# Eight row buffers for V in place of six, with a new instruction order, in a fused adaLN block of sliding attention and SwiGLU

## The chip, the cores and the metric

The kernel runs on one core of a Trainium2 chip. Five engines work beside one another and are ordered by semaphores alone: TensorE (PE in the profile, with its weight loads as PEld), VectorE (DVE), ScalarE (ACT), GpSimd (POOL) and SyncE (SP), which here issues nearly all DMA transfers. The metric is the device time of one execution in microseconds (us), the median of several runs.

## The reference

A transformer block on x of 2048 rows and 512 columns, in bfloat16, modulated by a conditioning vector c:

```python
mod = (silu(c) @ w_mod).reshape(1, 6, 1, 512)
sa, ca, ga, sb, cb, gb = mod[:, 0], ..., mod[:, 5]
h = layernorm(x) * (1 + ca) + sa
x = x + ga * attention(h)              # @ wqkv, window, @ wo
h = layernorm(x) * (1 + cb) + sb
x = x + gb * ((silu(h @ w1) * (h @ w3)) @ w2)   # 512 -> 1792 -> 512
return x
```

The attention has 32 heads of 16 columns. Row s attends to the eight rows s, s − 2, ..., s − 14, those before row 0 masked, with a softmax over the eight.

## The kernel before

The rows lie in 16 tiles of 128, T = 0 to 15. One function, `_build`, records 1151 operations of all engines by number in the program's own order. Two tables then fix how they run. `ORDER` is a list of those numbers; split by engine, it is the order in which each engine executes its operations, and for SP the order in which transfers are issued. `SLOTS` gives, for each of 590 values that live in a pool of buffers, which buffer of the pool it takes. `Program.place` goes through `ORDER`, and where a value takes a buffer that another had, its first operation must wait for every user of the value before (`o.prev`). `Program.synchronize` turns these and the data dependences into semaphore waits. Nothing waits otherwise: an engine runs its list from first to last, and an operation that waits holds up all that stand behind it on that engine.

The pools that matter here: eight PSUM banks of 512 columns, which all products on TensorE share, three buffers for modulated rows `h`, four output buffers, and `vpool`, the row buffers `vb` for V.

The work, in groups that overlap:

- LayerNorm 1 and the projections to q, k and v go in row groups {0,1}, {2,3}, {4–7}, {8–11}, {12–15}. After the statistics, TensorE transposes the rows and ScalarE evacuates them with the modulation (line 673); for the last group a DMA transposes. Keys and queries come out transposed (product at line 722, evacuation on ScalarE at 730 to 734).
- V comes out with rows on the partitions (`proj_v`, line 749). A copy on ScalarE (line 759) reorders its columns into a buffer of `vpool`, and a DMA of 128 KB on SP stores that buffer into a scratch tensor in HBM, `v_scratch_dram`. The buffer can be written again when the store has landed.
- Attention goes by tile. VectorE multiplies q by eight shifted views of k (line 780); TensorE sums over each head's columns (line 791, in 32-column tiles of the array); the softmax runs on VectorE (803 to 840) with the exponential on ScalarE (821). Four DMA loads per tile (`values`) bring the eight shifted rows of V back from the scratch tensor, VectorE weights them (line 862), TensorE sums over the window (line 871), ScalarE copies the sum out (877), a DMA transposes it, TensorE multiplies by wo (895), and VectorE adds the result to x (899).
- LayerNorm 2 takes a square with accumulation on ScalarE (614), two small operations on GpSimd (620, 621), one on VectorE (622) and the normalization on ScalarE (625). DMA transposes it and ScalarE modulates it in place (648); for the first groups TensorE transposes.
- The feed-forward network goes in the same row groups, numbered 0 to 4. For each of 14 blocks f of 128 hidden columns TensorE makes a gate and an up product (line 911, four matmuls each), ScalarE takes silu of the gate (917) and, in groups 0 to 3, copies the up product out (921), and VectorE multiplies (922; from PSUM in group 4, line 925). The product with w2 (953; 941 for the last two tiles) and the addition on VectorE (969) end it, and a DMA stores the rows.

ScalarE holds one table of functions at a time: exp and silu each need a table load (ACT_TABLE_LOAD) where they follow the other. Both orders have eight loads.

The operation numbers that the text speaks of:

| operations | engine | what |
|---|---|---|
| 153, 159, 203, 207, 254, 257, 260, 263, 312, 315, 318, 321, 366, 369, 372, 375 | ACT | copies of V of tiles 0 to 15; each one's store is the next number, on SP |
| 403–406, 413–416 | SP | loads of the shifted V rows of tiles 0 and 1 |
| 49, 45, 44 | SP | weight load w3 (second part), gate and scale weights of the second modulation |
| 293, 294 and 295 | ACT, PE | last modulated rows of tiles 8 to 11; the first key product of tiles 12 to 15 behind them |
| 542, 543 | PE, ACT | window sum of tile 9, its copy out |
| 553 | ACT | exponential of the logits of tiles 10 and 11 |
| 911, 871, 881, 883, 866, 876, 873 | PE | gate and up products of FFN group 2 |
| 912, 884, 882 | ACT | silu of 911; up copy and silu of 883 and 881 |
| 1014, 1004 | ACT | up copies of group 3, f = 10 and f = 8 |
| 1057, 1062, 1061 | ACT | square of tile 15; normalization of tiles 15 and 14 |
| 1066, 1065, 826 | SP | the last two transposes of FFN group 4's rows; a store of output rows of tile 3 |

Of the kernel before, what the change touches and what calls it, by code (L numbers as in the profile page):

```python
# [10 lines left out]
P = 128  # L11
S = 2048
D = 512
# [267 lines left out]
def _build(p, A_x, A_wqkv, A_wo, B_w1, B_w3, B_w2, c, w_mod, out):  # L281
# [6 lines left out]
    def sb(shape, dtype, name):  # L288
        return ctx.enter_context(nc.sbuf_tensor("sb_" + name, shape, dtype))
# [11 lines left out]
    vb = [sb([P, D], bf, f"v{i}") for i in range(6)]  # L301
# [761 lines left out]
]  # L1063
SLOTS = [
# [45 lines left out]
```

## Time and profile before

| | before |
|---|---|
| median of 3 runs | 238.87 us (238.83 to 239.16) |
| the profiled execution | 239.86 us |
| its span in the profile | 237.7 us |
| granted clock of TensorE | 1.00 |
| instructions in the trace | 4314 |
| busy: PE, DVE, ACT, POOL | 229.9, 169.8, 156.4, 23.1 us |
| the sixteen stores of V, issue to landing | 3.0 at least, 5.8 median, 12.3 at most |

How to read it: the page counts an engine busy while an instruction runs and lists for each idle stretch what released it. A row of the timeline is start, duration, engine, line and operation, output <- inputs with shapes, the number of instructions merged into the row, and in square brackets the idle time ahead of it with its releaser. A row of the waits is the waiting engine and line, what it waited for, and then us in total, times and the longest. Each time in the text is of that one execution unless it says otherwise.

### The profile page before, as it was taken

How to read it: one execution, taken by the hardware profiler on the slowest of the kernel's cores; microseconds unless marked ns; L12 is line 12 of the kernel's file. 1: busy time of each engine (PE TensorE's matmuls, PEld its weight loads, DVE VectorE, ACT ScalarE, POOL GpSimd, SP SyncE). 2: the span in 40 equal slices, each digit the busy share in tenths (PEclk: the TensorE clock that was granted, in tenths of full speed). 3: DMA queues.
4: the chain of work that ended last, by engine and by line, in shares of the span. 5: the costliest groups of instructions: out<-in, count | busy, mean ns of one | idle time of the engine just before them, and what ended most of it. 6: DMA issues, size and time to landing. Idle time of an engine off the chain costs nothing.

```text
span 237.7 us, 4314 instructions
## 1 busy us (share of the span) xinstructions
PE 229.9 (97%) x1665; PEld 120.7 (51%) x1689; DVE 169.8 (71%) x284; ACT 156.4 (66%) x311; POOL 23.1 (10%) x55
## 2 busy tenths in 40 slices
PE   7899998999999999999999999999999999999996
PEld 2667543544568855754434444444344444444454
DVE  4789998999999999999999847379134424042722
ACT  2289798899989987683689799444757926133100
POOL 8323050001001000030000021000001100000000
PEclk9999999999999999999999999999999999999999
DMA  6999999989999977693897484330032142000002
GB/s 185 341 352 351 238 274 179 188 221 297 327 261 273 285 181 223 139 261 69 205 330 116 124 229 105 103 117 0 3 90 88 44 77 80 0 0 0 3 0 88
DMA packets 44731, 38.31 MB, mean 161 GB/s; under 512 B 19736, under 2 KB 36008, under 8 KB 44712
## 3 DMA queue, kind: packets, MB, share of 16 engines
q1 hardware_dynamic: 44656, 38.04, 63.3%
q8 instruction: 13, 0.21, 0.4%
q14 instruction: 6, 0.05, 0.1%
q10 hardware_dynamic: 56, 0.01, 0.0%
HBM read 29.63 MB, written 4.21 MB: 142 GB/s over the span
## 4 chain that ended last, share of the span: by engine, by line
PE 68%; DVE 12%; DMA 7%; ACT 7%; issue 3%; POOL 1%; SPq 1%; DVEq 0%
PE pall L911 38%; PE pall L953 13%; PE pall L722 5%; DMA sb_wo<-in_A_wo_dram 5%; PE pall L895 4%; DVE sb_vsh L862 3%; PE pall L941 3%; DMA sb_wm_s<-in_w_mod_dram 2%; PE pall L871 2%; PE pall L749 2%; ACT sb_h L648 1%; ACT sb_xn L614 1%; PE pall L791 1%; DVE sb_pq L780 1%; DVE sb_pq L862 1%
## 5 line engine op out<-in xcount | busy, mean ns | idle before, releaser
L911 PE MATMUL pall<-sb_h,sb_w 128*128 128x512 bf16 (+1 forms) x554 | 99.6, 336 | 0.5 <-issue 0.2
L911 PEld LDWEIGHTS pall<-sb_h,sb_w 128*128 128x128 bf16 x560 | 52.2, 98 | 47.1 <-ACT sb_sg L917 5.2
L917 ACT ACTIVATE sb_sg<-pall 128x512 bf16<-128x512 f32 (+1 forms) x70 | 33.9, 516 | 29.6 <-PE pall L911 28.6
L953 PE MATMUL pall<-sb_w,sb_hh 128*128 128x512 bf16 x190 | 43.4, 379 | 0.3
L722 PE MATMUL pall<-sb_h,sb_wqkv 128*128 128x512 bf16 (+1 forms) x157 | 30.4, 336 | 1.3 <-ACT sb_v L759 0.8
L953 PEld LDWEIGHTS pall<-sb_w,sb_hh 128*128 128x128 bf16 x196 | 18.9, 98 | 22.7 <-issue 0.4
L921 ACT ACTIVATE sb_hh<-pall 128x256 bf16<-128x256 f32 (+1 forms) x56 | 26.8, 497 | 3.4 <-PE pall L911 3.0
L922 DVE TENSOR_TENSOR sb_hh<-sb_sg,sb_hh 128x256 bf16<-128x256 bf16 (+1 forms) x56 | 17.7, 351 | 12.8 <-ACT sb_hh L921 12.8
L969 DVE TENSOR_TENSOR sb_o<-pall,sb_x 128x512 bf16<-128x512 f32 (+3 forms) x18 | 10.9, 627 | 18.5 <-PE pall L953 13.7
L722 PEld LDWEIGHTS pall<-sb_h,sb_wqkv 128*128 128x128 bf16 x160 | 14.6, 98 | 14.0 <-ACT sb_v L759 1.3
L925 DVE TENSOR_TENSOR sb_hh<-sb_sg,pall 128x512 bf16<-128x512 bf16 x14 | 9.1, 684 | 16.0 <-PE pall L911 15.9
L648 ACT ACTIVATE sb_h<-sb_h,sb_modc 128x512 bf16<-128x512 bf16 x16 | 11.7, 806 | 11.2 <-DMA sb_h<-sb_xn 11.2
L620 POOL TENSOR_SCALAR sb_rs<-sb_var 128x2 f32<-128x2 f32 x8 | 3.4, 427 | 144.4 <-ACT sb_xn L614 144.4
L862 DVE TENSOR_TENSOR sb_pq<-sb_pq,sb_al 128x4096 bf16<-128x4096 bf16 x7 | 15.8, 2285 | 1.0 <-DMA sb_pq<-v_scratch_dram 1.0
L862 DVE TENSOR_TENSOR sb_vsh<-sb_vsh,sb_al 128x4096 bf16<-128x4096 bf16 x7 | 15.9, 2281 | 0.0
L749 PE MATMUL pall<-sb_wqkv,sb_h 128*128 128x512 bf16 x59 | 15.2, 379 | 0.3 <-issue 0.2
L895 PE MATMUL pall<-sb_wo,sb_ot 128*128 128x512 bf16 x60 | 14.9, 379 | 0.6 <-issue 0.5
L673 ACT ACTIVATE sb_h<-pall,sb_modc 128x256 bf16<-128x256 bf16 (+1 forms) x20 | 12.2, 659 | 2.7 <-DVE sb_modc L522 1.8
L780 DVE TENSOR_TENSOR sb_vsh<-sb_q,sb_kT 128x4096 bf16<-128x4096 bf16 x6 | 13.6, 2286 | 0.4 <-ACT sb_q L730 0.4
L625 ACT ACTIVATE sb_xn<-sb_x,sb_nb,sb_rs 128x512 bf16<-128x512 bf16 x16 | 12.4, 818 | 1.9 <-DVE sb_nb L622 1.7
L614 ACT ACTIVATE sb_xn<-sb_x,sb_nm 128x512 bf16<-128x512 bf16 x16 | 11.4, 716 | 2.7 <-DVE sb_nm L610 2.7
L899 DVE SCALAR_TENSOR_TENSOR sb_x<-pall,sb_x 128x512 bf16<-128x512 f32 x16 | 10.7, 678 | 2.9 <-PE pall L895 2.7
(111 smaller groups left out, 254.5 us busy)
## 6 DMA issues: line engine op xcount, KB each, us to landing
sb_pq<-v_scratch_dram SPq DMA_DIRECT2D x28, 256.0 KB, 6.8
sb_vsh<-v_scratch_dram SPq DMA_DIRECT2D x28, 256.0 KB, 5.0
sb_w<-in_B_w_dram SPq DMA_DIRECT2D x6, 512.0 KB, 6.9
sb_w<-in_B_w_dram SPq DMA_DIRECT2D x6, 384.0 KB, 5.9
v_scratch_dram<-sb_v SPq DMA_DIRECT2D x16, 128.0 KB, 5.8
out_dram<-sb_o SPq DMA_DIRECT2D x14, 128.0 KB, 1.8
sb_wqkv<-in_A_wqkv_dram SPq DMA_DIRECT2D x6, 256.0 KB, 6.2
sb_x<-in_A_x_dram SPq DMA_DIRECT2D x3, 512.0 KB, 7.7
```

The lines of the kernel that those rows point to most:

```text
L614: p.op("act", lambda e, vn=vn, T=T: e.activation(vn.at[:], x_sb[:, T, :], ACT.Square, bias=nm[:, T, :], scale=D ** -0.5, accum_out=var[:, ...
L648: return e.activation(vh.at[:, ft, 0:n * P], vh.at[:, ft, 0:n * P], ACT.Identity, bias=modc[:, 8 * which + ft:8 * which + ft + 1], scale=m ...
L722: ins = e.matmul(bank(vp)[:, 0:n], wqkv[:, t, kind * D + ft * P:kind * D + (ft + 1) * P], vh.at[:, t, 0:n], start=(t == ORDER[0]), stop=(t ...
L749: ins = e.matmul(bank(vp), vh.at[:, t, tt * P:(tt + 1) * P], wqkv[:, t, 2 * D:3 * D], start=(t == ORDER[0]), stop=(t == ORDER[-1]))
L780: return e.tensor_tensor(bass.AP(vp.at, 0, [[8 * D, P], [KT * P, W], [P, KT], [1, P]]), in0, in1, ALU.mult)
L862: return e.tensor_tensor(v_w, v_w, a_w, ALU.mult)
L895: ins = e.matmul(bank(vy), vt.at[:, ft, :], wo[:, ft, :], start=(ft == 0), stop=(ft == KT - 1))
L911: ins = e.matmul(bank(vp)[:, 0:n], wt[:, t, fi * P:(fi + 1) * P], vh.at[:, t, 0:n], start=(t == 0), stop=(t == KT - 1))
L917: p.op("act", lambda e: e.activation(vt.at[:, 0:n], bank(vgp)[:, 0:n], ACT.Silu), c_act(n), k, r=[vgp], w=[vt], table="silu")
L921: p.op("act", lambda e: e.activation(vh_.at[:, 0:n], bank(vup)[:, 0:n], ACT.Copy), c_act(n), k, r=[vup], w=[vh_])
L922: p.op("dve", lambda e: e.tensor_tensor(vh_.at[:, 0:n], vt.at[:, 0:n], vh_.at[:, 0:n], ALU.mult), 60 + n * 69 // 128, k, r=[vt], w=[vh_], ...
L953: ins = e.matmul(bank(vz), vhh[fi].at[:, tt * P:(tt + 1) * P], w2[:, fi, :], start=(fi == 0), stop=(fi == NF - 1))
```

## The change

The list of V buffers has eight entries in place of six, and `ORDER` and `SLOTS` are replaced whole by another search's result, for which the landings of those stores had been put longer. The operations recorded are the same 1151 in both, and so are their shapes; only the order on each engine and the buffer of each value differ. The copies of V run in the tile order 1, 0, 2, 3, 7, 4, 6, 9, 10, 5, 8, 11, 14, 13, 12, 15 before the change and 1, 0, 2, 4, 6, 3, 7, 9, 5, 11, 10, 8, 14, 13, 12, 15 after it.

```diff
-    vb = [sb([P, D], bf, f"v{i}") for i in range(6)]
+    vb = [sb([P, D], bf, f"v{i}") for i in range(8)]
...
 ORDER = [
...
-    212, 209, 150, 151, 217, 155, 156, 152, 157, 175, 158, 159, 153, 109, 114, 9, 180, 181, 154, 41, 49, 210, 192, 129, 195, 186, 187, 160,
-    44, 198, 130, 201, 182, 218, 40, 144, 405, 220, 265, 188, 145, 45, 267, 42, 266, 139, 202, 203, 146, 147, 213, 183, 184, 140, 185, 196,
-    197, 199, 404, 148, 141, 221, 193, 194, 131, 132, 133, 134, 200, 416, 214, 215, 216, 226, 225, 222, 224, 228, 223, 227, 230, 189, 177,
...
-    208, 262, 263, 264, 248, 284, 392, 394, 393, 39, 283, 290, 291, 395, 425, 286, 287, 292, 250, 288, 294, 326, 327, 239, 240, 293, 204,
-    396, 335, 397, 398, 54, 252, 243, 241, 242, 423, 237, 238, 254, 245, 295, 314, 399, 384, 259, 336, 400, 337, 338, 340, 339, 328, 401,
-    297, 343, 329, 330, 341, 331, 402, 385, 417, 260, 261, 303, 299, 379, 315, 301, 380, 305, 300, 342, 52, 407, 302, 244, 246, 381, 344,
...
-    613, 614, 993, 625, 626, 936, 1047, 924, 973, 1049, 990, 974, 1048, 994, 1050, 1027, 1051, 995, 985, 1010, 1052, 1013, 966, 968, 975,
-    969, 1054, 637, 1022, 967, 627, 628, 1023, 1024, 928, 1003, 638, 1012, 1055, 1028, 1064, 1056, 1057, 1058, 1059, 970, 1053, 1039, 1035,
-    1043, 1031, 1025, 1063, 1014, 1004, 1060, 1062, 1066, 826, 1061, 1029, 1015, 1065, 1070, 1069, 1030, 1005, 1036, 1044, 1037, 1068, 1032,
...
+    172, 157, 109, 126, 209, 119, 201, 202, 152, 186, 158, 42, 114, 124, 159, 160, 180, 211, 210, 219, 212, 198, 217, 153, 154, 41, 45, 181,
+    44, 182, 183, 184, 139, 405, 185, 134, 416, 187, 213, 214, 220, 189, 195, 192, 188, 203, 193, 194, 218, 221, 135, 406, 40, 413, 144,
+    199, 200, 222, 267, 215, 231, 145, 146, 196, 197, 147, 216, 226, 223, 233, 225, 224, 234, 148, 232, 235, 227, 404, 415, 276, 274, 265,
+    275, 277, 278, 414, 279, 228, 229, 205, 206, 129, 190, 236, 177, 130, 136, 137, 266, 230, 131, 132, 133, 403, 178, 140, 334, 141, 142,
+    268, 269, 270, 143, 377, 179, 191, 138, 259, 253, 254, 247, 323, 325, 378, 280, 241, 249, 271, 273, 272, 282, 289, 49, 54, 284, 260,
+    290, 250, 242, 332, 392, 281, 394, 393, 283, 243, 248, 425, 395, 396, 285, 244, 207, 208, 291, 286, 287, 288, 245, 292, 294, 326, 335,
...
+    548, 551, 581, 542, 731, 535, 543, 552, 825, 373, 536, 560, 571, 727, 553, 554, 561, 569, 911, 912, 871, 728, 881, 570, 370, 826, 883,
+    884, 866, 882, 876, 568, 873, 874, 872, 891, 555, 556, 877, 557, 582, 885, 868, 869, 562, 376, 630, 544, 584, 892, 851, 893, 861, 863,
...
+    962, 963, 964, 1009, 1054, 1064, 1011, 998, 1012, 965, 1010, 1053, 1063, 924, 999, 1013, 1001, 1018, 1019, 1000, 1002, 1003, 1043, 1014,
+    1015, 1020, 1004, 1035, 1005, 1036, 732, 1039, 1040, 1057, 1058, 1059, 1060, 1062, 1066, 1041, 1061, 1065, 1069, 1067, 1037, 1031, 1032,
...
 SLOTS = [
...
```

99 rows, old and new, of tables (ORDER, SLOTS) are left out of this document.

## The prediction, made before the changed kernel was built

> **What bounds the kernel now.** I read the head of the page first, then the share of the engines in seven stretches, then the waits and the stretches around the longest of them. The head says how full each engine is, and the page's fourth part what the chain that ends last consists of.
>
> ```profile
> span 237.7 us, 4314 instructions
> PE 229.9 (97%) x1665; PEld 120.7 (51%) x1689; DVE 169.8 (71%) x284; ACT 156.4 (66%) x311; POOL 23.1 (10%) x55
> PE 68%; DVE 12%; DMA 7%; ACT 7%; issue 3%; POOL 1%; SPq 1%; DVEq 0%
> ```
>
> TensorE is busy for 229.9 of 237.7 us, so all that any reordering can win is 7.8 us, and most of that lies where no buffer of V plays a part: in the next table 2.34 us before 14 us and 2.48 us after 199 us. Its columns are the stretch, its length, the busy time of PE, PEld, DVE, ACT and POOL, the granted clock, the DMA share and GB/s.
>
> ```profile
> 0.00:14.00 14.00, 11.66 (x105) 6.08 (x106) 7.77 (x29) 4.98 (x10) 7.05 (x27) 1.00 0.88 276
> 14.00:42.00 28.00, 26.94 (x228) 15.80 (x230) 26.48 (x46) 24.81 (x50) 6.93 (x12) 1.00 1.12 273
> 42.00:62.00 20.00, 19.69 (x227) 10.44 (x229) 19.63 (x22) 18.85 (x37) 1.23 (x2) 1.00 1.03 250
> 62.00:116.00 54.00, 52.99 (x479) 34.75 (x486) 52.93 (x83) 42.40 (x101) 3.85 (x6) 1.00 0.89 215
> 116.00:157.00 41.00, 40.68 (x225) 17.75 (x229) 30.07 (x53) 31.90 (x54) 2.15 (x4) 1.00 0.69 179
> 157.00:199.00 42.00, 41.68 (x214) 17.89 (x217) 19.74 (x36) 25.78 (x48) 1.85 (x4) 1.00 0.21 46
> 199.00:237.70 38.70, 36.22 (x193) 18.00 (x194) 13.15 (x22) 7.71 (x14) 0.00 (x0) 1.00 0.07 24
> ```
>
> From 42 to 116 us VectorE is as full as TensorE (19.63 of 20 and 52.93 of 54), so time must be won on both there. After 116 TensorE alone is full, with 0.32 us idle in each of two stretches. ScalarE is full only from 42 to 62 (18.85 of 20). What the V buffers cost now stands in the waits, and in the timeline around 38 us:
>
> ```profile
> DVE sb_pq L862 <- DMA sb_pq<-v_scratch_dram: 1.0, 1, 1.0
> ACT sb_v L759 <- DMA v_scratch_dram<-sb_v: 0.8, 1, 0.8
> PE pall L722 <- ACT sb_v L759: 0.8, 1, 0.8
> ```
> ```profile
> 37.64 4.49 DVE L862 TENSOR_TENSOR sb_pq<-sb_pq,sb_al 128x4096 bf16<-128x4096 bf16 x2 [1.01 <-DMA sb_pq<-v_scratch_dram]
> ...
> 39.56 0.60 ACT L759 ACTIVATE sb_v<-pall 128x512 bf16<-128x512 f32 x1 [0.84 <-DMA v_scratch_dram<-sb_v]
> ...
> 40.21 1.90 PE L722 MATMUL pall<-sb_h,sb_wqkv 128*128 128x512 bf16 x8 [0.80 <-ACT sb_v L759]
> ```
>
> One copy of sixteen waits for a store: that of V tile 9, whose buffer still feeds the store of tile 7, and the key projection behind it waits 0.80 us for the bank. Beside it VectorE waits 1.01 us for the shifted V rows of tile 1. These two are what the change can remove.
>
> **The change, part by part.** *The buffers.* Two more buffers are memory and cost no time. Followed through the new buffer numbers, tile 9's copy waits for no store, nor does that of tile 10. But tiles 4 and 6 now come early and wait for the stores of tiles 0 and 1; eight buffers therefore don't end the waits, they move them. Eight copies now reuse a buffer whose store must have landed, where ten did. Copies and stores stay sixteen each.
>
> *The V loads at the start.* SP issues in order. These are the rows of its queue, of the stores, and of the copies (count | busy, mean ns | idle before):
>
> ```profile
> 16.35 0.58 SPq L127 DMA_DIRECT2D sb_w<-in_B_w_dram  x1
> ...
> 22.54 4.45 SPq L127 DMA_DIRECT2D sb_pq<-v_scratch_dram  x7
> ```
> ```profile
> v_scratch_dram<-sb_v SPq DMA_DIRECT2D x16, 128.0 KB, 5.8
> ```
> ```profile
> DMA to landing us min/median/max: 3.0/5.8/12.3
> ```
> ```profile
> L759 ACT ACTIVATE sb_v<-pall 128x512 bf16<-128x512 f32 x16 | 9.7, 613 | 2.2 <-PE pall L749 1.3 <-DMA v_scratch_dram<-sb_v 0.8
> L917 ACT ACTIVATE sb_sg<-pall 128x512 bf16<-128x512 f32 x42 | 24.1, 597 | 27.9 <-PE pall L911 27.9
> ```
>
> In the old order a weight load (op 49, issued at 16.35) goes ahead of all eight V loads of tiles 0 and 1; in the new one it goes behind them. The loads then land earlier, and I take the whole wait on VectorE as gone: −1.0, between −1.01 and 0 (0 if the stores, now tile 1 before tile 0 at SP, set the loads' start). The store wait at tile 9 lies on TensorE in a stretch where VectorE is just as full, so beside the −1.0 it gives 0, at the most −0.8. Next late on VectorE is then the residual addition of tile 1, behind this product, which the change doesn't move forward on TensorE:
>
> ```profile
> 48.41 1.89 PE L895 MATMUL pall<-sb_wo,sb_ot 128*128 128x512 bf16 x8
> ```
>
> It may give part of the −1.0 back; the terms that follow stand for that. Of the stores, that of tile 7 (264) falls from place 35 to 65 in SP's queue. The first load that reads it stands 13 places on; at 0.6 of SP's time each (the 0.58 row) that is 7.8 us, more than the median landing of 5.8, so 0 here.
>
> *ScalarE before 42 us.* Ahead of the last modulated rows of tiles 8 to 11 (op 294) stand two V copies (254, 260) and two key evacuations more and one V copy (263) less: 1.93 us by their own durations. The gaps there that could take it up are these:
>
> ```profile
> 27.25 0.60 ACT L759 ACTIVATE sb_v<-pall 128x512 bf16<-128x512 f32 x1 [0.40 <-PE pall L749]
> ...
> 29.22 0.78 ACT L673 ACTIVATE sb_h<-pall,sb_modc 128x512 bf16<-128x512 bf16 x1 [0.89 <-PE pall L663]
> ```
>
> 0.40 + 0.89 = 1.29, which leaves 0.64 for TensorE's key projection (295) to wait; between 0 and +0.64, I take +0.4, as the copies are also pulled out of later ScalarE work. The copy 254 now comes where ScalarE stood at 23.4 us; a store issued like tile 1's at 17.0 lands by the median at 17.0 + 5.8 = 22.8, by the longest at 29.3. Early by 0.6 or late by 5.9: I take +0.3, close to the median. By 115 us the sum is −1.0 + 0.4 + 0.3 = −0.3.
>
> *FFN group 2 (tiles 4 to 7).* This is the largest cost I find. The rows at its start:
>
> ```profile
> 112.94 2.93 ACT L648 ACTIVATE sb_h<-sb_h,sb_modc 128x512 bf16<-128x512 bf16 x4 [3.47 <-DMA sb_h<-sb_xn]
> ...
> 114.50 0.62 PE L791 MATMUL pall<-sb_vshx,sb_E 128*32 128x256 bf16 x16 [0.28 <-DVE sb_vshx L780]
> ...
> 115.93 2.33 PE L911 MATMUL pall<-sb_h,sb_w 128*128 128x512 bf16 x10
> ```
>
> Now TensorE enters the group at 115.93, 0.06 after ScalarE's last modulation (112.94 + 2.93 = 115.87). In the new order its first gate (911) takes the bank of the attention sum of tile 9 (542), and the copy that empties it (543) is queued on ScalarE behind that modulation. One copy, 0.60, and the hand-over of 0.06 come on top: 0 if the modulation ends that much before TensorE is ready, +0.66 if not. VectorE's product for tile 9 is now the last before it, at the place of the 114.50 row, so TensorE isn't ready early; I take +0.5. Behind 543 stand the exponential (553) and both table loads:
>
> ```profile
> 86.42 1.28 ACT L821 ACT_TABLE_LOAD   x1
> 87.71 0.58 ACT L821 ACTIVATE pall<-pall 128x512 f32<-128x512 f32 x1
> 88.30 1.28 ACT L917 ACT_TABLE_LOAD   x1
> ```
> ```profile
> 157.18 9.07 PE pall L911 x42
> ```
>
> 1.28 + 0.58 + 1.28 + three evacuations of 0.60 make 4.94 us from the end of copy 543. TensorE issues six products of four matmuls at 9.07/42 = 0.216, that is 6 × 0.864 = 5.18 us, before it needs the bank of the third one freed. So that costs nothing, with 0.24 to spare.
>
> The Trainium skill (ScalarE: Activation LUTs, What ACT_TABLE_LOAD costs) puts a switch of tables at 1283 ns of load and a drain of 1380 ns behind it. The trace shows the 1.28, and the exponential 1.29 after the load began, so no drain of that size is exposed here; by the page the 4.94 would be 7.70 and the sum 2.5 us higher.
>
> *FFN groups 3 and 4.* The rows around the last group's start:
>
> ```profile
> 188.28 2.86 SPq L127 DMA_TRANSPOSE sb_h<-sb_xn  x2
> 191.18 0.58 SPq L127 DMA_DIRECT2D out_dram<-sb_o  x1
> 191.80 1.20 SPq L127 DMA_TRANSPOSE sb_h<-sb_xn  x1
> ```
> ```profile
> 186.74 0.72 ACT L614 ACTIVATE sb_xn<-sb_x,sb_nm 128x512 bf16<-128x512 bf16 x1
> ...
> 188.15 1.07 ACT L921 ACTIVATE sb_hh<-pall 128x512 bf16<-128x512 f32 x2
> 189.10 1.52 ACT L625 ACTIVATE sb_xn<-sb_x,sb_nb,sb_rs 128x512 bf16<-128x512 bf16 x2
> ...
> 195.82 2.93 ACT L648 ACTIVATE sb_h<-sb_h,sb_modc 128x512 bf16<-128x512 bf16 x4 [4.71 <-DMA sb_h<-sb_xn]
> ```
> ```profile
> 198.81 1.47 PE L911 MATMUL pall<-sb_h,sb_w 128*128 128x512 bf16 x6
> ```
>
> The last group's rows are ready at 195.82 + 2.93 = 198.75 and TensorE starts at 198.81: no slack. In the new order the two evacuations of the 188.15 row (1014, 1004) go ahead of the square of tile 15 (1057, at 186.74), which puts the chain up to 1.07 later. Against that, the store issued at 191.18 between the last two transposes has moved ahead of both, which gives back 0.62. I take +0.2, between 0 and +1.07. In group 3 six or so first uses of a bank follow its evacuation by less than 0.1 us where the old order left more; I take +0.2 for them, between 0 and +0.6. In group 4 one up product (1125, f = 13) needs a bank freed by a multiplication that ends, by my addition, 0.07 after it; +0.1, between 0 and +0.3. The sixteen output stores are spread anew; the last four still follow the last four additions, so 0 there.
>
> **Sum.** −0.3 + 0.5 + 0.2 + 0.2 + 0.1 = +0.7 us on the profiled execution, 239.86 us (span 237.7 and 2.16 around it). That execution is 0.99 above the median of 238.87; the same step on the median gives 239.6 us.
>
> **Rivals.** *Faster, 237.9 us.* The V loads' mechanism: the 1.01 us at 37.64 goes whole and VectorE, full to 116 us, carries it to FFN group 2, whose modulated rows come 1.0 earlier and leave ScalarE time for copy 543. 238.87 − 1.0. For it speaks 52.93 of 54 on VectorE; against it that 0.06 us at 115.93 and 198.81 bind from ScalarE and that TensorE has 0.32 idle in the next 41 us, nothing to catch up with. It decides if more than 0.7 of the 1.01 is left at 116 us.
>
> *No change, 238.9 us.* Group 2's extra 0.5 is hidden, since copy 543 finds ScalarE free, and the −0.3 pays for the ties: −0.3 + 0 + 0.3. For it speaks that no work is added.
>
> *Clearly slower, 241.0 us.* The store wait doesn't go, it comes back where ScalarE is fullest. V tile 12 (copy 366) takes the buffer of tile 8 (copy 312, store 313); between the two copies ScalarE has 6.4 us of work, and the landing takes 5.8 by the median, 12.3 at the longest. From 6.4 on each us is one on ScalarE, and the 39.56 and 40.21 rows show that 0.84 there became 0.80 on TensorE. A landing of 7.8 adds 1.4: 239.6 + 1.4. Against it: the median is 0.6 below the point from which it counts.
>
> *The drain.* With tables as that page prices them, 4.94 becomes 7.70, TensorE waits 2.5 us in group 2, and the time is 239.6 + 2.5 = 242.1 us. The row of 87.71 speaks against it.
>
> **How the numbers follow.** Forecast (a little slower, 239.6, own range 239.35 to 240.4) 0.36; faster 0.27; no change 0.20; store wait back 0.15; drain 0.02. Within ±0.2% (0.48 us), about what a measurement of this kernel can tell from no change, is 238.4 to 239.35. Slower is 0.36 + 0.15 + 0.02 = 0.53. The range goes from 237.7 (all of the 1.01 and 0.2 of the 0.80 kept) to 241.9 (the upper ends 0.64, 0.66, 1.07, 0.6 taken together without the gain: 238.87 + 2.97), which leaves out the drain and tails of the outer two.
>
> **What would show it.** After the change the wait at tile 9 and the 1.01 on VectorE should be gone, and the first weighted V product of tile 1 start before 37 us. TensorE's first gate of group 2 should wait for the copy of an attention sum; if it waits for the modulation instead, and starts before 115.3, the faster rival holds. A store wait of over 0.5 us at any V copy between 42 and 62 us is the slower rival. If TensorE reaches its last group after 199.2, the chain of tile 15 was mispriced. I am wrong if the waits before 42 us that go were worth more than VectorE shows, or if ties by the dozen, which I priced at 0.3, add up to more.

## The result and the profile after

The changed kernel takes 241.94 us (median of 4 runs, 241.65 to 242.21) against 238.95 us before (238.83 to 239.16): slower by 1.24%, ratio 1.0124 with a 95% interval of 1.0106 to 1.0142. Forecast were 239.6 us and a range up to 241.9. The direction was right, the size was not: +3.0 us where +0.7 was forecast. The profiled execution of the changed kernel took 242.21 us, 2.35 above the one of before; the remaining 0.6 us of the 3.0 can't be read from these two traces, since the profiled execution of before lay 0.9 above its own median; the last part of the experiments comes back to it. Three single runs of the later comparisons, more than 1.5% above the fastest of their kernel, are left out of the ratios.

The head of the page and the stretches after the change (stretch, its length, busy time of PE, PEld, DVE, ACT and POOL, clock, DMA share, GB/s):

```profile
span 240.0 us, 4332 instructions
PE 232.1 (97%) x1689; PEld 120.3 (50%) x1689; DVE 170.5 (71%) x284; ACT 156.1 (65%) x311; POOL 26.1 (11%) x55
```
```profile
14.00:42.00 28.00, 28.00 (x279) 16.57 (x277) 27.37 (x47) 26.43 (x53) 7.61 (x12) 1.00 0.98 268
42.00:62.00 20.00, 19.33 (x197) 9.29 (x189) 18.93 (x21) 17.27 (x34) 1.99 (x2) 1.00 0.90 266
62.00:116.00 54.00, 53.56 (x484) 34.13 (x476) 52.54 (x83) 42.05 (x101) 5.52 (x6) 1.00 0.82 203
...
157.00:199.00 42.00, 40.60 (x211) 17.33 (x210) 18.35 (x35) 23.66 (x47) 1.85 (x4) 1.00 0.23 43
```

TensorE is busy without a gap from 14 to 42 us now (28.00, before 26.94), and it has lost 1.08 us between 157 and 199 us (40.60, before 41.68). The trace of before lacks 24 matmul records (1665 against 1689), which shortens its busy time somewhat, so I used a second measure: the start of a TensorE operation less the nominal time of all TensorE operations ahead of it in its order (0.216 per matmul of 512 columns, 0.44 per sum in the tiled mode). That lag grows only where TensorE stands still. The first matmul of the first v product and of op 535 is among the missing records, here and in the trace of every experiment but e13; there the start is put one matmul (0.22) ahead of the first record that is left. Op 307 is a query product, op 439 the window sum of tile 2, op 535 the wo product of tile 8. Worked out from the starts in the traces, in us:

```
                       first v  q op 307  sum 439  op 535  first of  first of  first of  last
                       product  (50 us)   (62 us)  (115)   group 2   group 3   group 4   matmul
before                   2.92     5.07      5.46    7.17     7.18      7.62      7.92     8.02
after                    2.95     4.13      5.18    7.25     8.02      8.20     10.30    10.29
```

The change is 0.94 ahead at 50 us, 0.28 at 62 and level at 115 (7.25 and 7.17), loses 0.76 around the start of FFN group 2, and then 1.8 more between the first product of group 3 and the first of group 4 (2.10 against 0.30). The last lags differ by 2.27, the spans by 2.3.

The waits of the changed kernel that answer to those shown of before, and the timeline of group 3:

```profile
ACT sb_oa L877 <- DMA sb_ot<-sb_oa: 3.3, 2, 1.8
...
PE pall L911 <- ACT sb_oa L877: 2.0, 2, 1.4
...
PE pall L722 <- ACT sb_v L759: 0.7, 1, 0.7
```
```profile
166.18 1.11 ACT L877 ACTIVATE sb_oa<-pall 128x512 bf16<-128x512 f32 x2
...
167.31 2.52 SPq L127 DMA_TRANSPOSE sb_ot<-sb_oa  x2
...
169.70 0.60 ACT L877 ACTIVATE sb_oa<-pall 128x512 bf16<-128x512 f32 x1 [1.52 <-DMA sb_ot<-sb_oa]
...
172.61 0.60 ACT L877 ACTIVATE sb_oa<-pall 128x512 bf16<-128x512 f32 x1 [1.82 <-DMA sb_ot<-sb_oa]
...
173.26 2.98 PE L911 MATMUL pall<-sb_h,sb_w 128*128 128x512 bf16 x13 [1.40 <-ACT sb_oa L877]
```

The window sums of the last four tiles are copied out in the order 13, 14, 12, 15, into two buffers (`oab`, `range(2)`). The first two copies fill both; a DMA transposes each buffer, and only when a transpose has landed can the next copy write into its buffer. So the copy of tile 12 waits 1.52 us and that of tile 15 another 1.82, and the up product 1008, which takes the PSUM bank that the sum of tile 15 leaves, stops TensorE for 1.40. Before, the order was 12, 13, 15, 14, the copies ran from 170.73 to 176.71, and TensorE waited for none of them:

```profile
170.73 0.60 ACT L877 ACTIVATE sb_oa<-pall 128x512 bf16<-128x512 f32 x1 [0.83 <-PE pall L871]
...
172.17 0.62 ACT L877 ACTIVATE sb_oa<-pall 128x512 bf16<-128x512 f32 x1
...
174.81 0.60 ACT L877 ACTIVATE sb_oa<-pall 128x512 bf16<-128x512 f32 x1
...
176.12 0.59 ACT L877 ACTIVATE sb_oa<-pall 128x512 bf16<-128x512 f32 x1
```

### The profile page after: what moved, and what is told of

The parts are those of the page before. It is cut to its first block, busy times and chain, and to the rows that moved or that the text cites. A ratio compares the mean times of both kernels' runs of the same rounds, so it can differ in the third digit from the quotient of the medians.

```text
span 240.0 us, 4332 instructions
## 1 busy us (share of the span) xinstructions
PE 232.1 (97%) x1689; PEld 120.3 (50%) x1689; DVE 170.5 (71%) x284; ACT 156.1 (65%) x311; POOL 26.1 (11%) x55
## 5 line engine op out<-in xcount | busy, mean ns | idle before, releaser
L911 PE MATMUL pall<-sb_h,sb_w 128*128 128x512 bf16 (+1 forms) x560 | 101.1, 337 | 2.1 <-ACT sb_oa L877 2.0
L953 PE MATMUL pall<-sb_w,sb_hh 128*128 128x512 bf16 x196 | 44.0, 379 | 0.0
L722 PE MATMUL pall<-sb_h,sb_wqkv 128*128 128x512 bf16 (+1 forms) x160 | 31.3, 337 | 0.7 <-ACT sb_v L759 0.7
L921 ACT ACTIVATE sb_hh<-pall 128x256 bf16<-128x256 f32 (+1 forms) x56 | 25.9, 495 | 5.8 <-PE pall L911 5.7
L620 POOL TENSOR_SCALAR sb_rs<-sb_var 128x2 f32<-128x2 f32 x8 | 5.7, 712 | 144.0 <-ACT sb_xn L614 144.0
L780 DVE TENSOR_TENSOR sb_vsh<-sb_q,sb_kT 128x4096 bf16<-128x4096 bf16 x9 | 20.3, 2277 | 0.0
L749 PE MATMUL pall<-sb_wqkv,sb_h 128*128 128x512 bf16 x64 | 16.0, 380 | 0.0
L895 PE MATMUL pall<-sb_wo,sb_ot 128*128 128x512 bf16 x64 | 16.0, 380 | 0.0
L862 DVE TENSOR_TENSOR sb_pq<-sb_pq,sb_al 128x4096 bf16<-128x4096 bf16 x6 | 13.6, 2287 | 2.2 <-DMA sb_pq<-v_scratch_dram 2.2
L877 ACT ACTIVATE sb_oa<-pall 128x512 bf16<-128x512 f32 x16 | 9.4, 607 | 6.2 <-DMA sb_ot<-sb_oa 3.3
```

The costliest lines, as they stand in the source:

```text
L722: ins = e.matmul(bank(vp)[:, 0:n], wqkv[:, t, kind * D + ft * P:kind * D + (ft + 1) * P], vh.at[:, t, 0:n], start=(t == ORDER[0]), stop=(t ...
L749: ins = e.matmul(bank(vp), vh.at[:, t, tt * P:(tt + 1) * P], wqkv[:, t, 2 * D:3 * D], start=(t == ORDER[0]), stop=(t == ORDER[-1]))
L780: return e.tensor_tensor(bass.AP(vp.at, 0, [[8 * D, P], [KT * P, W], [P, KT], [1, P]]), in0, in1, ALU.mult)
L862: return e.tensor_tensor(v_w, v_w, a_w, ALU.mult)
L895: ins = e.matmul(bank(vy), vt.at[:, ft, :], wo[:, ft, :], start=(ft == 0), stop=(ft == KT - 1))
L911: ins = e.matmul(bank(vp)[:, 0:n], wt[:, t, fi * P:(fi + 1) * P], vh.at[:, t, 0:n], start=(t == 0), stop=(t == KT - 1))
```

## The experiments

My theory after this: the loss sits in waits that the new order makes with its buffers and banks, above all that of group 3, and not in the eight V buffers. The rivals: that these waits only show where TensorE would have waited anyway, and that the V buffers or their memory cost something. The ratios below are to the kernel before, run beside each; there the runs of one kernel spread over 1.4 to 3.6 us, so that intervals are ±0.25 to 0.36%, and I go by the lags too, each of one execution. All kernels, in the table's columns:

```
                        first v  q op 307  sum 439  op 535  group 2  group 3  group 4  last   ratio
e1 before, v9             2.76     3.98      4.51    6.23     6.23     6.67     7.16    7.26  0.9999
e7 before, load 49        3.22     4.44      5.61    7.33     7.36     7.81     8.11    8.21  0.9972
e11 before, both          4.10     5.30      6.08    7.79     7.80     8.23     9.04    9.14  1.0004
e13 the same again        2.76     3.95      4.35    6.30     6.31     6.75     7.13    7.18  1.0007
e8 after again            2.97     4.63      5.68    8.30     8.31     8.48    10.86   10.90  1.0097
e2 after, bank group 3    3.87     5.06      6.10    8.19     8.88     9.05     9.67    9.71  1.0090
e3 after, bank group 2    2.97     4.47      5.52    8.00     8.00     8.17    10.46   10.50  1.0111
e4 after, v14 first       2.97     4.14      5.27    7.33     7.34     7.51     9.52    9.56  1.0103
e6 after, these three     2.70     4.02      5.07    7.24     7.46     7.63     9.59    9.63  1.0038
e9 after, sum buffers     2.97     4.73      5.77    8.14     8.47     8.65     9.28    9.32  1.0025
e10 e9 with e3, e4        2.96     4.75      6.32    9.53     9.86    10.03    11.00   11.03  1.0036
e12 after, load 49 back   2.98     4.14      5.19    8.69     8.90     9.08    11.12   11.16  1.0077
```

**e1: the buffers alone, in the old order.** The new order itself can't be run with six: up to eight V copies stand in its list ahead of the stores that free their buffers.

```diff
-    vb = [sb([P, D], bf, f"v{i}") for i in range(6)]
+    vb = [sb([P, D], bf, f"v{i}") for i in range(8)]
 SLOTS: V tile 9: 1 -> 6
```

> The kernel before with eight V buffers and its own order; only V tile 9 takes a buffer of its own. If the store wait of 0.84 us at that copy is worth what TensorE waited for it (0.80 us), the time is 238.1 us. If VectorE bounds the stretch from 42 to 116 us, as the prediction had it, the time stays at 238.9 within 0.3 us. If eight buffers as such cost something (placement in memory), it is above 239.4.

Ratio 0.9999 (0.9974 to 1.0024). The store wait is gone from the trace, and the lag at the query product 307 falls from 5.07 to 3.98, at the last matmul from 8.02 to 7.26. But VectorE's wait of 1.01 us for V rows is gone too, which the edit doesn't touch:

```profile
36.46 4.49 DVE L862 TENSOR_TENSOR sb_pq<-sb_pq,sb_al 128x4096 bf16<-128x4096 bf16 x2
```

Apart from where the buffers lie in memory, the edit first acts at tile 9's copy, which comes behind that wait. What differs ahead of it is the landings. The store of tile 7 was issued at 27.87 us in the trace of before and landed at 39.53; in e1 it was issued at 27.72 and landed at 37.19. The last load that VectorE waited for landed at 37.54 in before, at 35.32 in e1. The trace gained 0.8 on that of before, the median nothing that could be measured. Eight buffers as such cost nothing that an interval of ±0.25% (0.6 us) would show.

**e2, e3, e4: one wait of the new order each.** e2 and e3 exchange two PSUM banks for all values from one operation on, e4 moves two normalizations on ScalarE.

```diff
 e2, SLOTS from op 1008 on: bank 3 <-> bank 6
 e3, SLOTS from op 911 on:  bank 3 <-> bank 5
 e4, ORDER:
-    ... 644, 645, 646, 371, 485, 372, 448, ...
+    ... 644, 371, 485, 372, 645, 646, 448, ...
```

> The changed kernel, same order; from the up product 1008 of FFN group 3 on, PSUM banks 3 and 6 are exchanged, so that 1008 doesn't take the bank of the window sum of tile 15. If that bank is what TensorE lost 1.40 us for at 173 us, the time falls from 241.9 to 240.4 us. If the wait only shows where TensorE would have waited anyway (for the residual rows of tile 15 or for the last group's modulated rows), the time stays within 0.4 us of 241.9.

> The changed kernel, same order; from the first gate product 911 of FFN group 2 on, banks 3 and 5 are exchanged, so that 911 doesn't take the bank of the window sum of tile 9. If ScalarE's copy of that sum is what TensorE waits 0.60 us for at 116.8 us, the time falls to 241.3 us. If the evacuations behind the exponential and the two table loads then stop TensorE some 5 us later instead, or the second wait at 173 us takes it up, it stays within 0.3 us of 241.9.

> The changed kernel; on ScalarE the V copy of tile 14 goes ahead of the two normalizations of tiles 0 and 1, for which ScalarE waits 1.43 us on VectorE and GpSimd. If TensorE's 0.67 us at 57 us is caused by these normalizations ahead of the copy and not by a store, that wait is gone; the time falls to 241.3 us if the gain lasts to the end, and stays within 0.3 us of 241.9 if VectorE sets the pace up to 116 us.

e2 gives 1.0090 (1.0058 to 1.0122): no clear gain in time, though in its trace the step from group 3 to group 4 fell from 2.10 to 0.62. e3 gives 1.0111 (1.0075 to 1.0147): its trace has no stop of TensorE at group 2 (8.00, then 8.00), and group 3 takes 2.29. But e4 and e8 keep the old bank there and show no stop either (7.33, then 7.34; 8.30, then 8.31), so e3 doesn't show that the exchange removed it. e4 gives 1.0103 (1.0067 to 1.0139) and shows what stood behind the normalizations. Its ScalarE, before 58 us:

```profile
55.32 0.60 ACT L759 ACTIVATE sb_v<-pall 128x512 bf16<-128x512 f32 x1 [1.62 <-DMA v_scratch_dram<-sb_v]
55.81 1.51 ACT L625 ACTIVATE sb_xn<-sb_x,sb_nb,sb_rs 128x512 bf16<-128x512 bf16 x2
```

Put first, V tile 14's copy waits 1.62 us for the store of tile 6, whose buffer it takes. The store wait had therefore not gone with eight buffers; in the changed kernel that store landed at 54.52 us, while ScalarE waited for VectorE:

```profile
55.12 1.52 ACT L625 ACTIVATE sb_xn<-sb_x,sb_nb,sb_rs 128x512 bf16<-128x512 bf16 x2 [1.43 <-DVE sb_nb L622]
...
56.54 0.57 ACT L759 ACTIVATE sb_v<-pall 128x512 bf16<-128x512 f32 x1
...
57.17 1.04 PE L722 MATMUL pall<-sb_h,sb_wqkv 128*128 128x512 bf16 x4 [0.67 <-ACT sb_v L759]
```

**e5 and e9: the buffers of the window sums.** Four buffers in place of two didn't fit in memory, so that e5 gave no result:

> The changed kernel, same order and same PSUM banks; four buffers in place of two for the copies of the window sums, so that the copies of tiles 12 and 15 don't wait for the DMA transposes of tiles 14 and 13. If those transposes are the root of TensorE's 1.40 us at 173 us, that wait goes and the time falls by about 1.5 us against the changed kernel run beside it (e8), as in e2. If ScalarE's order of work is the root, the copy of tile 15 comes no earlier and nothing changes.

e9 lends two V buffers that are free by then:

```diff
-    oab = [sb([P, D], bf, f"oa{i}") for i in range(2)]
+    oab = [sb([P, D], bf, f"oa{i}") for i in range(2)] + vb[6:8]
 SLOTS: sum of tile 12: 1 -> 2, of tile 15: 0 -> 3
```

> The changed kernel, same order and banks; the copies of the window sums of tiles 12 and 15 take two V buffers (6 and 7), which are free by then, in place of the two buffers that the DMA transposes of tiles 14 and 13 still read. If those transposes hold ScalarE's copies and through them TensorE between 168 and 174 us, both waits of ScalarE on a transpose go, TensorE's lag grows by less than 0.4 us in FFN group 3 in place of 1.6 to 2.4, and the time falls to some 240.4 us (1.0% over the kernel before becomes 0.4%). If the banks alone are to blame, nothing changes.

Ratio 1.0025 (1.0000 to 1.0050), against 1.0097 (1.0063 to 1.0131) for the changed kernel measured again (e8, below): 0.7% or 1.7 us back, a little more than expected. The trace:

```profile
166.59 1.11 ACT L877 ACTIVATE sb_oa<-pall 128x512 bf16<-128x512 f32 x2
...
168.49 0.59 ACT L877 ACTIVATE sb_v<-pall 128x512 bf16<-128x512 f32 x1
...
169.92 0.59 ACT L877 ACTIVATE sb_v<-pall 128x512 bf16<-128x512 f32 x1
...
171.25 1.03 PE L895 MATMUL pall<-sb_wo,sb_ot 128*128 128x512 bf16 x4
```

All four copies are done by 170.51, none waits for a transpose, and group 3 costs 0.63 of lag, not less than 0.4 as expected, but far from the 2.10 and 2.38 of the changed kernel. By itself this trace wouldn't settle it, since both transposes landed early in it (2.36 and 2.40 us after their issue). The median of twelve runs does, together with e10 below: there the first transpose took 4.08 us, as in the bad cases, and group 3 still costs only 0.97. So the two buffers are the root of the largest loss.

**e8: the changed kernel again, and e6: the three edits of e2, e3 and e4 together.**

> The changed kernel as it is, on the same chip as e5 to e7. 241.9 us where the chip runs as steadily as in the first comparison; 1.0 to 1.4% above the kernel before in any case. Its trace should again show TensorE's waits at 57, 117 and 173 us.

> The changed kernel with three edits together: the bank exchange of e3 at FFN group 2, that of e2 at group 3, and the V copy of tile 14 ahead of the normalizations (e4). If the changed kernel's loss lies in these three waits (0.67, 0.60 and 1.40 us on TensorE) and its start is really 0.9 us ahead, the time is 2.7 us below that of e8, near 239.2 us and level with the kernel before. If TensorE is held by something common behind them, it gains no more than e2 alone, about 1.5 us.

e8's trace differs from the first one in which wait is long:

```profile
171.85 0.60 ACT L877 ACTIVATE sb_oa<-pall 128x512 bf16<-128x512 f32 x1 [3.43 <-DMA sb_ot<-sb_oa]
172.82 0.60 ACT L877 ACTIVATE sb_oa<-pall 128x512 bf16<-128x512 f32 x1
...
172.50 1.04 PE L895 MATMUL pall<-sb_wo,sb_ot 128*128 128x512 bf16 x4 [1.26 <-ACT sb_oa L877]
```

Here the first transpose landed late, so the copy of tile 12 waited the whole 3.43 us and the wo product that takes its bank stopped TensorE; group 3 cost 2.38 in all. The wait at 57 us is there again (0.7). Group 2 cost nothing, copy 543 being done in time: the wait that I had forecast there is only in some executions. e6 gives 1.0038 (1.0006 to 1.0070), 0.6% or 1.4 us below e8 where 2.7 was expected if the three waits were all, and yet its profiled execution shows 1.96 in group 3 by that same wait for the first transpose; most of its lead over e8 there lies ahead of op 535 (7.24 against 8.30). So the bank exchange of e2 helps only where that transpose lands early, and which of its three edits won the 1.4 us isn't shown; more buffers help in both cases.

**e10: e9 with the edits of e3 and e4.**

> As e9, with the bank exchange of e3 (FFN group 2) and the V copy of tile 14 ahead of the normalizations (e4). If the three places are independent and each on TensorE's path, the time is 2.5 us below the changed kernel: level with the kernel before or up to 0.4 us faster, the start being 0.9 us ahead. If ScalarE or VectorE sets the pace behind them, it is no better than e9.

Ratio 1.0036 (1.0005 to 1.0067), no better than e9. Its trace is of an execution 2.1 us above its median, so the large lags in the table don't stand for the kernel. In it, and in that of e12, another wait appears at 72 to 78 us, which e8 and e9 don't have: VectorE waits at the scaling of a part of w2 (line 996) for its load, and a multiplication, a silu with its up copy and a gate product wait behind it. Three rows of e12's waits between 70 and 78 us:

```profile
DVE sb_w L996 <- DMA sb_w<-in_B_w_dram: 1.5, 1, 1.5
ACT sb_sg L917 <- DVE sb_hh L922: 1.5, 1, 1.5
PE pall L911 <- ACT sb_hh L921: 1.4, 1, 1.4
```

**e7, e11, e13: the two waits removed from the old order; e12: one of them put back into the new.**

```diff
 e7, ORDER of before: 49 from behind 41 to behind 406
 e11 and e13: e7 with e1
 e12, ORDER of after: 49 from behind 289 to ahead of 405
```

> The kernel before, same buffers; only the weight load 49 is issued behind the V loads of tiles 0 and 1, as in the new order. If that load is what made VectorE wait 1.01 us at 37.6 us, the wait is gone; the time is 1.0 us lower if VectorE carries the gain to 116 us (the faster rival), and within 0.4 us of the kernel before if the store wait of V tile 9, which stays, or the last group's start takes it back.

> The kernel before with its own order, and only the two edits that answer the two waits read off its profile: V tile 9 in a buffer of its own (eight buffers), and the weight load 49 behind the V loads of tiles 0 and 1. If the store wait and the load wait are both on the path, 0.8 to 1.8 us faster than before (238.0 or less); if the one covers the other, about as e7, 0.7 us faster; if TensorE finds its next limit at the last group's start, less than 0.5 us.

> The kernel of e11 once more: the old order with V tile 9 in a buffer of its own and the weight load 49 behind the first V loads. e7 came out 0.28% faster and e11, which holds e7's edit, level; the traces put both edits together at 0.8 to 1.0 us less by 57 us. If that reaches the end, the ratio is 0.996 to 0.998; if TensorE's last group starts by ScalarE's rows anyway, it is 0.999 to 1.001, as in e11.

> The changed kernel with the weight load 49 back ahead of the V loads of tiles 0 and 1. If the new order's start is ahead because of that load, VectorE waits for V rows again before 42 us and TensorE's lead of 0.9 us at 50 us is gone; at the end of the kernel that shows as 0 to 1.0 us, depending on whether the later waits swallow it. If the lead comes from the order on ScalarE and TensorE, it stays.

e7 comes out at 0.9972 (0.9947 to 0.9997), e11 at 1.0004 (0.9978 to 1.0030), and e13, the same program as e11, at 1.0007 (0.9973 to 1.0041). e7's interval ends just below 1, but it is one of twelve comparisons, and e11 and e13, which hold its edit, come out level: no version is shown to beat the kernel before, and the gain that was expected of e11 did not come. And e7, whose buffers are those of before, has no store wait at tile 9 either; its copies of tiles 6 and 9 run without a gap:

```profile
38.40 1.13 ACT L759 ACTIVATE sb_v<-pall 128x512 bf16<-128x512 f32 x2
```

So each of the two edits came with the loss of both waits. The landings explain it. The store of tile 7, issued between 27.7 and 29.5 us, landed at 39.53 in the trace of before and at 39.74 in e11, but at 37.19, 37.67 and 36.75 in e1, e7 and e13. (In e11 tile 9 has a buffer of its own, and no copy waits for that store. e7 has six V buffers and e11 eight, so their place in memory isn't what makes it late.) The two waits of before thus go with transfers that landed some two us later than in e1, e7 and e13, and not with the order alone. How often the kernel before has them isn't shown, as it was profiled once. That its profiled execution lay 0.9 above the first median says little: beside the experiments the same kernel took 239.97 to 240.30 us in the median.

The lags agree. From the first v product to op 307 they grow by 2.15 in before, by 1.19 to 1.22 in the four other traces of the old order, and by 1.16 to 1.79 in those of the new one. So the lead of 0.94 at 50 us comes from the late landings in one execution of before, and is no gain of the new order. Nor does it come from the place of the weight load: e12 gives 1.0077 (1.0042 to 1.0112), not told apart from e8, no wait for V rows comes back before 42 us, and at op 307 it lags 4.14, as the changed kernel does.

## Why the prediction was right or wrong

*Up to 115 us, −0.3: not borne out.* The lag at op 535 is level with that of before (7.25 and 7.17). Both waits of before are gone, but e1, e7, e11 and e13 don't bear out that the buffers took the one and the moved load the other: the old order ran without either in e1 and in e7, and no ratio is below 0.997. The −1.0 was read off an execution with late landings, which doesn't stand for the median. Against e1, whose 239.1 us in its profiled execution is close to the 238.95 of before, the changed kernel is 1.0 behind at op 535 (7.25 and 6.23) and 3.0 behind at the last matmul (10.29 and 7.26), as much as the medians differ. What I had not priced is the wait at 57 us, ScalarE's 1.43 for VectorE with a copy of V behind it, which cost TensorE 0.67. The +0.4 and +0.3 for ScalarE before 42 us didn't come: TensorE is 28.00 of 28 busy.

*FFN group 2, +0.5 (0 to 0.66): the mechanism was there.* TensorE's first gate waited 0.60 for copy 543, which ran behind the modulation, and the lag grew by 0.76, a little more than the upper bound:

```profile
116.14 0.57 ACT L877 ACTIVATE sb_oa<-pall 128x512 bf16<-128x512 f32 x1
...
116.73 1.28 ACT L821 ACT_TABLE_LOAD   x1
116.77 2.55 PE L911 MATMUL pall<-sb_h,sb_w 128*128 128x512 bf16 x11 [0.60 <-ACT sb_oa L877]
...
118.02 0.58 ACT L821 ACTIVATE pall<-pall 128x512 f32<-128x512 f32 x1
...
118.62 1.28 ACT L917 ACT_TABLE_LOAD   x1
```

The two table loads and the exponential cost TensorE nothing, as worked out. The exponential begins 1.29 after its load and the next load 0.60 after that, so the drain of 1380 ns that the Trainium skill puts behind each load (ScalarE: Activation LUTs, What ACT_TABLE_LOAD costs) is not exposed here either; that rival is out. In the other traces with the same bank the wait for copy 543 was 0.5 (e2), 0.2 (e9) or absent (e4, e8, e12).

*FFN group 3, +0.2 (0 to 0.6): this is the step that failed.* The term "first uses of a bank follow its evacuation by less than 0.1 us" counted only ScalarE's own work ahead of each evacuation. The evacuation itself had to wait for a buffer that a DMA transpose was still reading. Measured: 1.8 more than before in the first trace, where 0.2 was forecast and 0.6 the upper bound; over the changed kernel and all its variants with two sum buffers but e2, the step is 1.96 to 2.38, with four it is 0.63 (e9) and 0.97 (e10), before 0.30.

*The chain to the last group, +0.2: about right.* From the stop at 173 us to the group's first product the lag grows by 0.28, over the same part of before by 0.12. TensorE reaches that group at 201.20, behind the 199.2 that I had named as the sign of a mispriced chain, but the stops ahead of it did that. *Group 4, +0.1:* nothing (10.30, then 10.29).

*The rivals.* "Faster" had its gain from VectorE's wait of 1.01, and where both waits were taken away in the old order (e11, e13) nothing came of it: 1.0004 and 1.0007. "Store wait back" had the mechanism, a V copy waiting for a store where ScalarE is full, but at tile 14 instead of 12 and of little weight: taking the normalizations out of its way (e4) won nothing. The drain is refuted by the rows above. The range ended 0.04 below the result, since its upper end held no price for a buffer pool other than V's. That it came so near is luck: of the upper ends that it added up, the 0.64 came to nothing and the 1.07 to some 0.2, while the 0.66 came to 0.76 and the 0.6 to 1.8.

*Left open:* 0.25% (0.6 us) stays in e9. Between 62 and 115 us its lag grows by 2.37, that of the changed kernel by 2.07 and 2.62 in two traces, that of the old order by 1.71 to 1.95 in five; I didn't test which wait that is.

## What to carry to other kernels

Where an order is replaced whole, follow every small pool through it, not only the one that the change names: for each first use of a buffer or bank, ask what the operation that frees it waits for in its turn, to the DMA if it ends there; a pool of two whose buffers go through a transfer of 2.3 to 4.3 us, as here, bears two uses close together and no third. A wait read off a single execution may not be there in the next, so compare the landings behind it in a second profile of the same kernel before you price the wait as a gain. A table of one engine's lag at a dozen marks shows in one look where each part was won and lost.

## What the runs showed of the hardware

*A transpose's landing varies.* SP issued the transposes of two sums 1.25 us apart each time. In the changed kernel they landed 2.37 and 4.03 us after their issue (167.31 to 169.68, 168.56 to 172.59), in e8 4.28 and 3.54, in e9 2.36 and 2.40. Which of the two is late decides which of the two stops of TensorE occurs: the wo product stopped where the first was late (e3, e6, e8, e12), product 1008 where the second was (the changed kernel, e4). What makes one late isn't shown.

*TensorE's start moves whole executions by over a microsecond.* e11 and e13 are one program; their spans are 238.8 and 236.9, and 1.34 of these 1.9 us are there already at the first v product (4.10 and 2.76 in the table). The warm-up products show it. First e11, then e13:

```profile
7.53 1.01 PE L542 MATMUL pall<-sb_ones 128*128 128x512 bf16 x2
```
```profile
7.20 0.59 PE L542 MATMUL pall<-sb_ones 128*128 128x512 bf16 x2
```

Two matmuls that take 0.59 at full speed take 1.01 in e11 at 7.5 us, 6 us after the first. The profile gives the granted clock as 1.00 in both, but that is a mean over what the clock's record covers, and the record in the trace begins at 10.6 us in e11, at 5.1 in e13 and at 4.3 in the changed kernel, each time about where the products turn fast. The Trainium skill (TensorE: Matmul & The Clock Gate, Part 1) says that the gate opens after a busy window of some 3.4 us that runs freely, so that the same kernel has more or fewer slow matmuls each time. The traces agree that it varies: in the changed kernel the products are fast from 4.4 us on, 2.9 us after the first, in e11 not yet at 8.6, 7.1 us after the first. The recorded stretches at full clock fit such a window too: they last 228.69 us in e11, 232.11 in e13 and 235.52 in the changed kernel, in steps of 3.41. Why it took e11 so long isn't shown.
